# Softmax weights as exp(w - ln of the sum) on ScalarE, tap sums on TensorE in a reordered prologue, and a tiled linear rest, in a fused convolution and maxout kernel

## The chip, the cores and the metric

The kernel runs on one core of a Trainium2 chip. The metric is the device time of one execution in microseconds (us), given as a median over several executions. The core has five engines, each of which is given its instructions in program order: TensorE (PE in the profile, its weight loads PEld), VectorE (DVE), ScalarE (ACT), GpSimd (POOL) and SyncE (SP, which here only issues DMAs). Each execution is classed as fast or slow against the others of its kernel.

## The reference, cut to what matters

```python
w = np.exp(weight_gen - max)                      # (8, 4160, 8 heads, 7 taps)
w = w / (sum over taps + 1e-09)
out[b,s,h,:] = sum over k of w[b,s,h,k] * x_pad[b, s + k, h, :]     # 24 values per head
y  = out.reshape(33280, 192)
h1 = y @ w1                                       # 192 -> 1024
h2 = y @ w2
return np.maximum(h1, h2) @ w_out                 # 1024 -> 192
```

Both kernels use max(h1, h2) = h1 + relu(h2 - h1). They multiply y by wd = w2 - w1, take the relu, multiply by w_out, and add y times w10 = w1 @ w_out, which is a linear path of width 192. The inputs are small enough that neither subtracts the maximum.

## The kernel before

A sequence is laid out over 16 partitions, so that each of the 128 partitions holds 260 consecutive positions ("columns"). Work goes in chunks of 16 columns, and each chunk in two units of 8 for TensorE. Per chunk ScalarE does one exp. VectorE does the sums, the reciprocal, the weights written in pairs, the product with seven shifted copies of x, and three adds. A DMA transposes y. TensorE then runs, for a unit, four "slots", each with two of the eight slices of the hidden layer and two output columns of the unit before it.

```python
def exp(ci):
    ...
    nc.scalar.activation(out=e_t, in_=wg_ts.pop(ci), func=AF.Exp)

def conv(ci):
    ...
    nc.vector.reduce_sum(out=sum_t, in_=_sub(e_t, 0, [[K, TH], [1, K]]), axis=AX.X)
    nc.vector.reciprocal(out=rec_t, in_=sum_t)
    nc.vector.tensor_tensor(                                   # weights, each twice
        out=_sub(en_t, 0, [[2, TH], [2 * TH, K], [1, 2]]),
        in0=_sub(e_t, 0, [[K, TH], [1, K], [0, 2]]),
        in1=_sub(rec_t, 0, [[1, TH], [0, K], [0, 2]]), op=ALU.mult)
    nc.vector.tensor_tensor(out=m_t, in0=..., in1=..., op=ALU.mult)   # the product
    if ci + 2 < len(CHUNKS):
        load(ci + 2)
    ...                                                        # three adds, y_t
...
def out_first(u, i):                                           # the linear rest
    ...
    nc.tensor.matmul(op[:, 0:2 * D], lhsT=yt[:, (3*i + 1)*P:(3*i + 2)*P], rhs=w10R, ...)
...
for u in range(NU + 1):
    while queued < NCH and queued <= UNITS[min(u + 3, NU - 1)][0]:
        exp(queued)                                            # three units ahead
        conv(queued)
        queued += 1
    if u == 0:
        transpose(0)
    if u + 1 < NU:
        transpose(u + 1)
    for i in range(4):
        ...                                                    # one slot
```

The exp of a chunk is issued three units before TensorE needs it.

The softmax here doesn't subtract the row's maximum and nothing guards it: scores larger than these inputs give would overflow.

## Time and profile before

The time is 477.56 us (three runs, 477.13 to 477.79). The table gives, for the profiled execution, what the argument uses; the prediction shows the lines themselves and says how to read them.

| | busy us | share of the 476.3 us span |
|---|---|---|
| TensorE | 427.1 | 90% |
| VectorE | 418.6 | 88% |
| ScalarE | 336.5 | 71% |
| time of one chunk of 16 columns on VectorE | 25.61 | |
| time of one chunk on TensorE, when it doesn't wait | 25.25 | |

A share near 100% after the prologue on two engines at once means that neither can be helped alone: shortening one gains at most the difference to the other.

### The profile page before, as it was taken

To read this page: it belongs to the slowest core of one execution; us is meant where nothing else is said; L and a number is where in the kernel's file an instruction comes from. 1 tells how busy PE (TensorE), PEld (TensorE's weight loads), DVE (VectorE), ACT (ScalarE), POOL (GpSimd) and SP (SyncE) were. 2 spreads that over 40 slices of the span, in tenths; PEclk is the share of its full clock that TensorE was granted. 3 is DMA by queue.
4 is the path that set the end of the run, shared out by engine and by line. 5 is a ranking of instruction groups with operands and counts; after the bars stand their busy time and mean duration, and the time that the engine had idled before them with its cause. 6 is when DMAs were issued, how large, how long until landed. Compare 5 with 4: busy or idle time off the path is not lost.

```text
span 476.3 us, 8155 instructions
## 1 busy us (share of the span) xinstructions
PE 427.1 (90%) x3606; PEld 271.5 (57%) x3606; DVE 418.6 (88%) x136; ACT 336.5 (71%) x437; POOL 22.1 (5%) x46
## 2 busy tenths in 40 slices
PE   0087695599999999999999999989999999999997
PEld 0054353366666666666666666656666666666675
DVE  2949999999999999999999999999999999997000
ACT  1266374287877878787878787867878787777773
POOL 3000000000000000000000000000000000000000
PEclk9999698599999999999999999999999999999999
DMA  8945745546574737467585747384736537273212
GB/s 168 261 107 104 170 120 129 133 93 169 131 175 123 199 107 174 150 139 190 131 200 125 206 85 219 76 192 109 200 109 139 172 67 200 43 200 100 83 67 100
DMA packets 62131, 67.47 MB, mean 142 GB/s; under 512 B 52329, under 2 KB 53609, under 8 KB 60304
## 3 DMA queue, kind: packets, MB, share of 16 engines
q1 hardware_dynamic: 57792, 41.12, 31.1%
q0 software_dynamic: 4304, 25.84, 24.9%
q8 instruction: 28, 0.46, 0.4%
q14 instruction: 7, 0.06, 0.0%
HBM read 46.58 MB, written 25.56 MB: 151 GB/s over the span
## 4 chain that ended last, share of the span: by engine, by line
PE 81%; DVE 11%; DMA 5%; SPq 1%; ACT 1%; issue 0%; POOLq 0%
PE op_ps L292 34%; PE hdp L243 22%; PE hdp L258 13%; PE op_ps L279 7%; DVE m_t L138 5%; PE op_ps L287 4%; DMA wso<-in_moe_w_out_dram 3%; DVE m_t L149 2%; DMA yt<-y_t 2%; DVE m_t L151 1%; DVE en_t L130 1%; PE pw L211 1%; DVE y_t L154 1%; DMA wg_t<-in_weight_gen_dram 1%; DVE sum_t L125 1%; DVE rec_t L127 1%
## 5 line engine op out<-in xcount | busy, mean ns | idle before, releaser
L269 ACT ACTIVATE rd_t<-hdp 128x1024 bf16<-128x1024 f32 (+1 forms) x272 | 267.5, 986 | 112.0 <-PE hdp L258 77.2
L292 PE MATMUL op_ps<-wo,rd_t 128*128 128x192 bf16 x2080 | 216.6, 248 | 0.0
L292 PEld LDWEIGHTS <-rd_t 128*128 128x128 bf16 x2080 | 177.8, 99 | 23.7 <-issue 0.9
L138 DVE TENSOR_TENSOR m_t<-xb_t,en_t 128x21504 bf16<-128x21504 bf16 (+2 forms) x19 | 185.0, 9738 | 5.5 <-DMA xb_t<-zero_t 4.9
L243 PE MATMUL hdp<-yt,wdE 128*128 128x512 bf16 (+1 forms) x272 | 101.6, 374 | 20.8 <-DMA yt<-y_t 18.3
L243 PE MATMUL hdp<-yt,wdO 128*128 128x512 bf16 (+1 forms) x272 | 101.5, 373 | 0.0
L258 PE MATMUL hdp<-yt,wdR 64*128 64x512 bf16 (+1 forms) x544 | 81.6, 375 | 1.1 <-ACT rd_t L269 1.1
L149 DVE TENSOR_TENSOR m_t<-m_t 128x9216 bf16<-128x9216 bf16 (+2 forms) x19 | 81.0, 4263 | 0.7
L303 ACT COPY o_t<-op_ps 128x384 f32<-128x384 f32 x130 | 61.6, 474 | 2.5 <-PE op_ps L292 2.3
L151 DVE TENSOR_TENSOR m_t<-m_t 128x6144 bf16<-128x6144 bf16 (+2 forms) x19 | 55.0, 2894 | 0.7
L258 PEld LDWEIGHTS <-wdR 64*128 64x128 bf16 x544 | 16.2, 94 | 58.1 <-issue 57.5
L279 PE MATMUL op_ps<-w10R,yt 128*128 128x384 bf16 x130 | 44.0, 339 | 0.0
L279 PEld LDWEIGHTS <-yt 128*128 128x128 bf16 x130 | 12.4, 96 | 53.1 <-issue 52.8
L243 PEld LDWEIGHTS <-wdE 128*128 128x128 bf16 x272 | 26.8, 99 | 22.0 <-DMA yt<-y_t 19.6
L287 PEld LDWEIGHTS <-yt 128*128 128x128 bf16 x260 | 25.7, 99 | 14.8 <-issue 0.6
L130 DVE TENSOR_TENSOR en_t<-e_t,rec_t 128x1792 bf16<-128x1792 bf16 (+2 forms) x19 | 33.4, 1755 | 0.7
L287 PE MATMUL op_ps<-w10E,yt 128*128 128x192 bf16 x130 | 32.2, 248 | 0.0
L287 PE MATMUL op_ps<-w10O,yt 128*128 128x192 bf16 x130 | 32.2, 248 | 0.0
L154 DVE TENSOR_TENSOR y_t<-m_t 128x3072 bf16<-128x3072 bf16 (+2 forms) x19 | 29.0, 1527 | 0.7
L243 PEld LDWEIGHTS <-wdO 128*128 128x128 bf16 x272 | 26.8, 99 | 3.6 <-issue 3.4
L125 DVE TENSOR_REDUCE sum_t<-e_t 128x128 f32<-128x896 bf16 (+2 forms) x19 | 17.9, 944 | 9.9 <-ACT e_t L115 9.9
L105 POOL DMA_DIRECT2D xb_t<-in_x_dram x18 | 9.5, 529 | 333.4 <-DVE m_t L138 333.4
(29 smaller groups left out, 69.0 us busy)
## 6 DMA issues: line engine op xcount, KB each, us to landing
out_dram<-o_t SPq DMA_DIRECT2D x31, 768.0 KB, 3.9
xb_t<-in_x_dram POOLq DMA_DIRECT2D x14, 1056.0 KB, 7.8
wg_t<-in_weight_gen_dram POOLq DMA_DIRECT2D x14, 448.0 KB, 6.1
xb_t<-in_x_dram POOLq DMA_DIRECT2D x3, 672.0 KB, 7.9
wg_t<-in_weight_gen_dram POOLq DMA_DIRECT2D x4, 224.0 KB, 5.5
wso<-in_moe_w_out_dram SPq DMA_DIRECT2D x1, 768.0 KB, 13.5
out_dram<-o_t SPq DMA_DIRECT2D x2, 384.0 KB, 3.6
yt<-y_t SPq DMA_TRANSPOSE x34, 3.8
```

Of the source, the lines that this page charges most:

```text
L130: nc.vector.tensor_tensor(out=_sub(en_t, 0, [[2, TH], [2 * TH, K], [1, 2]]), in0=_sub(e_t, 0, [[K, TH], [1, K], [0, 2]]), in1=_sub(rec_t, ...
L138: nc.vector.tensor_tensor(out=m_t, in0=_sub(xb_t, 0, [[D, K], [1, n]]), in1=_sub(en_t, 0, [[2 * TH, K], [2, TH], [0, D // H // 2], [1, 2]] ...
L149: nc.vector.tensor_tensor(out=m_t[:, 0:3 * n], in0=m_t[:, 0:3 * n], in1=m_t[:, 3 * n:6 * n], op=ALU.add)
L151: nc.vector.tensor_tensor(out=rows(m_t, 2, 2, 0), in0=rows(m_t, 2, 2, 0), in1=rows(m_t, 5, 2, 1), op=ALU.add)
L154: nc.vector.tensor_tensor(out=y_t, in0=m_t[:, 0:n], in1=m_t[:, 2 * n:3 * n], op=ALU.add)
L243: nc.tensor.matmul(hd_ts[u, f][:, j * 512:j * 512 + N], lhsT=wd[kind][:, f * P:(f + 1) * P], rhs=_sub(yt_ts[u], 2 * j * P, [[3 * P, n // 2 ...
L258: nc.tensor.matmul(hd_ts[u, f][:, j * 512:j * 512 + N], lhsT=wd["R"][r, f * P:(f + 1) * P], rhs=_sub(yt_ts[u][r, :], P, [[3 * P, n // 2], ...
L269: nc.scalar.activation(out=_sub(rd_ts[u], f * 1024, [[512, 2], [1, N]]), in_=_sub(hd_ts.pop((u, f)), 0, [[512, 2], [1, N]]), func=AF.Relu,)
L279: nc.tensor.matmul(op[:, 0:2 * D], lhsT=yt[:, (3 * i + 1) * P:(3 * i + 2) * P], rhs=w10R, start=True, stop=False, skip_group_check=True,)
L287: nc.tensor.matmul(op[:, sl], lhsT=yt[:, (3 * i + 2 * j) * P:(3 * i + 2 * j + 1) * P], rhs=(w10E, w10O)[j], start=False, stop=False, skip_ ...
L292: nc.tensor.matmul(op[:, sl], lhsT=rd[:, f, j * 512 + i * P:j * 512 + (i + 1) * P], rhs=wo[:, f * D:(f + 1) * D], start=False, stop=(f == ...
L303: nc.scalar.copy(out=o_ts[u][:, 2 * i * D:2 * (i + 1) * D], in_=op_ts.pop((u, i))[:, 0:2 * D])
```

## The change

Its intent is to take work off both full engines and to start TensorE sooner. VectorE loses the reciprocal and the paired product: ScalarE takes ln of the sums, VectorE subtracts it from the logits, and ScalarE writes exp of the result, reading each value twice. TensorE's linear rest, one matmul with a half-zero weight of 384 columns, becomes two 64-row matmuls side by side. In the prologue the taps of the first 16 columns are summed by matmuls with the identity, which leave y already transposed. "Batch" below is a chunk of 16 columns, counted from 0. From batch 1 on, y goes by DMA transpose, one for each unit; batch 2 is the first whose product is done in one instruction.

```diff
-        nc.vector.reciprocal(out=rec_t, in_=sum_t)
-        nc.vector.tensor_tensor(out=_sub(en_t, ...), in0=_sub(e_t, ...), in1=_sub(rec_t, ...), op=ALU.mult)
+    def ln(b):
+        nc.scalar.activation(out=s_ts[b], in_=s_ts[b], func=AF.Ln)
+    def shift(b):                       # fp32, 896 elements
+        nc.vector.tensor_tensor(out=wg, in0=wg, in1=s_ts.pop(b), op=ALU.subtract)
+    def weights(b, part=None):          # part 0: taps 0 to 3, part 1: taps 4 to 6
+        nc.scalar.activation(out=..., in_=_sub(wg_ts[b], ..., [[1, k1 - k0], [K, N], [0, 2]]), func=AF.Exp)
 ...
+    def sum_transpose(u):               # prologue only
+        for k in range(nb):
+            for t in range(K):
+                nc.tensor.matmul(ps[:, k * P:(k + 1) * P], lhsT=m_ts[b][...], rhs=ident, ...)
 ...
-            op[:, 0:2 * D], lhsT=yt[:, (3 * i + 1) * P:(3 * i + 2) * P], rhs=w10R,
+        for j in range(2):
+            r = slice(64 * j, 64 * j + 64)
+                lhsT=yt_ts[u][r, (3 * i + 1) * P:(3 * i + 2) * P], rhs=w10[r, 2 * D:3 * D],
 ...
+    extras = {
+        (1, 0): lambda: (weights(1), start_mul_1(), load_x(2, 0, 16), load_wg(4, nc.gpsimd)),
+        ...
+        (2, 0): lambda: exp_sum(3),
+        (2, 1): rest_1,
+        (2, 3): lambda: transpose(4),
+        ...
+    }
+    def extra(u, i):                    # after slot i of unit u
+        ...
+        if i == 0 and second and b + 1 < NB:
+            c, w = b + 1, BATCHES[b + 1][1]
+            mul(c, 0)                   # then shift(c + 1), red(c + 2), the adds, the loads
+            ...
+        if i == 1 and u + 1 < NU:
+            transpose(u + 1)
+        if second and b + 2 < NB:       # second: the second unit of batch b
+            if i == 1:
+                weights(b + 2, 0)
+            if i == 3:
+                weights(b + 2, 1)
+        if second and i == 3 and b + 3 < NB:
+            ln(b + 3)
```

The evictions of the output are also grouped (four of 768 elements per batch in place of eight of 384).

## The prediction

> **What bounds the kernel now.** I read the busy shares first, then the busy time in slices and by stage, then the groups of instructions kept apart by shape, then the timeline around one wait. Busy shares and slices (tenths of each fortieth of the span):
>
> ```profile
> PE 427.1 (90%) x3606; PEld 271.5 (57%) x3606; DVE 418.6 (88%) x136; ACT 336.5 (71%) x437; POOL 22.1 (5%) x46
> ...
> PE   0087695599999999999999999989999999999997
> ...
> DVE  2949999999999999999999999999999999997000
> ...
> PEclk9999698599999999999999999999999999999999
> ```
>
> TensorE and VectorE are both full from about 90 us on, so the slices cannot say which of them sets the pace. The groups give the work of one chunk of 16 columns on VectorE (line, shapes, count, busy us, mean ns):
>
> ```profile
> L138 DVE TENSOR_TENSOR m_t<-xb_t,en_t 128x21504 bf16<-128x21504 bf16 x14 | 159.0, 11359 | 0.5
> ...
> L149 DVE TENSOR_TENSOR m_t<-m_t 128x9216 bf16<-128x9216 bf16 x14 | 69.4, 4958 | 0.5
> ...
> L151 DVE TENSOR_TENSOR m_t<-m_t 128x6144 bf16<-128x6144 bf16 x14 | 47.0, 3357 | 0.5
> ...
> L154 DVE TENSOR_TENSOR y_t<-m_t 128x3072 bf16<-128x3072 bf16 x14 | 24.6, 1758 | 0.5
> ...
> L130 DVE TENSOR_TENSOR en_t<-e_t,rec_t 128x1792 bf16<-128x1792 bf16 x14 | 28.4, 2025 | 0.5
> ...
> L125 DVE TENSOR_REDUCE sum_t<-e_t 128x128 f32<-128x896 bf16 x14 | 15.1, 1078 | 0.0
> ...
> L127 DVE RECIPROCAL rec_t<-sum_t 128x128 f32<-128x128 f32 x14 | 13.3, 953 | 0.5
> ```
>
> They sum to 25.49 us. In the timeline of VectorE the product L138 starts at 267.89, 293.51 and 319.12, so a chunk takes 25.61, with no waits. For TensorE I take its repeating slot (a unit of 8 columns has four, a chunk eight). The timeline of TensorE around the one late wait:
>
> ```profile
> 313.22 0.34 PE L279 MATMUL op_ps<-w10R,yt 128*128 128x384 bf16 x1
> ...
> 316.38 0.34 PE L279 MATMUL op_ps<-w10R,yt 128*128 128x384 bf16 x1
> ...
> 317.80 0.82 PE L292 MATMUL op_ps<-wo,rd_t 128*128 128x192 bf16 x8
> 320.38 0.39 PE L243 MATMUL hdp<-yt,wdE 128*128 128x512 bf16 x1 [1.76 <-DMA yt<-y_t]
> ```
>
> A slot is 316.38 - 313.22 = 3.16 us, a chunk 25.25. TensorE is 0.36 faster per chunk than what feeds it, so from its cold start at 88.41 (0.61 us matmuls in place of 0.38, some 3 us lost) it catches up until it waits at 320. **VectorE sets the pace**, by a hair, and the start costs about 50 us: at 88.41 only 24 of 260 columns are through, which at 12.6 us per 8 columns is 38 us of work. From y_t ready (315.04) to the first matmul on it (320.38) is 5.3 us; at 84.5 to 88.41 it is 3.9.
>
> **What the Trainium skill says.** "VectorE: DVE Perf Modes", section "The perf-mode tier table", gives bf16 tensor_tensor two elements per cycle, fp32 tensor_tensor and any reduce one. The trace agrees: at that page's 0.96 GHz, 21504 / 2 is 11.2 us (11.36 seen), and the reduce of 896 is 0.93 (1.08 seen). "ScalarE: Activation LUTs", section "What ACT_TABLE_LOAD costs", gives an ACTIVATE with immediates 186 ns + 0.833 ns per element, with 93 ns overlap between neighbours: 0.93 us for 896 (0.942 seen). Its section "Table sets: the hidden batching unit" puts exp and ln in one set, so Ln should add no reload; before has one load, no run yet shows two functions. "TensorE: Matmul & The Clock Gate", Part 1, has the clock fall to half after an idle window of 3.4 us. The trace agrees in kind: idle for 6.18 and 10.34 us was followed by about 6 us of 0.6 us matmuls, idle for 1.76 was not.
>
> **The change, per 16 columns.** VectorE loses the reciprocal (0.95) and the pairing product (2.03). It gains an fp32 subtract of 896 elements, one per cycle, estimated 1.08 like the reduce of the same size. Product and adds keep their element counts. So 25.61 - 2.98 + 1.08 = 23.7 us.
>
> TensorE: the 384-column linear matmul (about 0.165 us) becomes two 64-row matmuls of 192 columns side by side (about 0.082, the step of the 192-column ones). The mode switches stay (about 0.1 us each, two in a slot: L243 to L258 steps 0.31 in place of 0.21). Slot 3.16 - 0.08 = 3.08; eight are 24.6.
>
> ScalarE: 16 relus of 1.02, exp 0.94 and eight evictions of 0.474 were 21.1. Evictions become four of 768 elements, estimated 0.79 each; new are ln (128 elements, 0.29) and the paired exp in two parts (1024 and 768 elements: 1.04 and 0.83). Sum 22.7 us, below TensorE. But each extra stands just before a slot with an eviction, in order: relu, extra, relu, eviction, relu is 0.35 us late for its two buffers by my count, of which about 0.2 reaches TensorE. Two such inside a batch: 25.0 us.
>
> If that were all, TensorE would set 25.0 against 25.6: 0.6 x 14 = 8 us won.
>
> **The wait that I expect to take its place.** Before, the exp that starts VectorE's work for a chunk is issued three units ahead. In the change the weights of batch b+2 come from ScalarE after the last relu of batch b, and ScalarE runs in program order. Call F(b) the time when TensorE starts batch b, G(b) when it has issued it (F + 25.0). The last relu starts about 0.55 before G, the next activation 0.93 later, part two takes 0.83: weights ready at G(b) + 1.25. Then VectorE does 23.7 (product, the next batch's subtract, a reduce, adds over all 16 columns, so y comes out at the end). Then the transpose: 3.9. So F(b+2) = F(b) + 25.0 + 1.25 + 23.7 + 3.9 = F(b) + 53.85: **26.9 us per batch**, above TensorE (25.0) and VectorE (23.7). The loop does not depend on how the kernel starts. Every two batches TensorE waits 3.85 us and VectorE about 6.4. Fourteen batches cost 14 x (26.9 - 25.6) = 18 us more.
>
> **The prologue**, estimated from the durations of before. Loading 16 columns of weight_gen first gives exp at about 5.5, reduce, ln, subtract to 9.1, paired exp to 9.75, product of 4 columns (2.96) to 12.7. The seven taps then sum on TensorE (42 matmuls, 4 to 5 us cold) to 17.5. The matrices start at 7.7, not 6.9, but without the loads beside them, and land by 17 (21 before). VectorE subtracts to 18.5, the shifted copies via TensorE and ScalarE take to 21, one cast and one exp to 23. The hidden layer of unit 0 runs 23 to 28 (1.28 per two f, as unit 0 before; it was 31.4), then tap sums (3.4), transposes (3.5), copy (1.9), w1 w_out (2.0 and 0.65) to 39. Slot 0 of unit 1 ends with the paired exp: first half ready at about 42.7. From there VectorE has an unbroken 49 us: 5.8 + 5.1, reduce 1.1, 5.8, 1.1, 1.1, 5.1, then 11.4 + 2.2 + 10.2. It is free for batch 3 at 91.7, and batch 2 starts at about 90.5. Column 32 starts at about 88.4 + 12.6 + 3 = 104 before. So the prologue wins some 13.5 us.
>
> **Sum.** F(3) = 91.7 + 23.7 + 3.9 = 119.3. F(15) = 119.3 + 6 x 53.85 = 442.4. G(15) = 467.4. The last 4 columns: four slots of 0.86 + 1.56 = 9.7, the last output 3.2, eviction and store 3.4 as now: 483.7, and 1.2 for the time above the span: 484.9. Roughly, -13.5 from the start, +18 from the loop, +3 as the tail no longer runs on a lead of three units.
>
> **Rivals.** (1) TensorE stays full at 25.0, because the weights come early enough or I misread which batch they serve. For it: a scheduler who saw the waits would have removed them, and one wait hides in slack easily. Against it: exp in the trace of before starts at 255.69, 280.93 and 306.22, in program order at the unit where it is issued. This gives 484.9 - 27 = 458. (2) The waits of 3.85 us exceed the 3.4 us idle window often enough to halve the clock: up to 3 us more for each of six, 490 to 500. The 1.76 us wait that did no harm says little here. (3) ScalarE becomes the bound, through reads of 0-stride pairs slower than one per cycle: double the 1.9 us and relu falls behind, 495. The VectorE pairing product, with such reads, kept 1792 / 0.96 = 1.87 (2.03 seen), which speaks against. (4) The loads of the prologue land late: each us there moves the end by one.
>
> **Range and chances.** The loop gives 485, give or take 5 for the prologue and 6 for six loops (1 us each: transpose 3.0 to 5.3, slot 3.05 to 3.15). I weigh it 4 to 1 against rival 1, so I set 482 and a range of 462 to 496. Faster than 468: almost only rival 1, 0.22. Slower than 487.1: 0.32. Between: 0.46.
>
> **What would show it.** Right: TensorE waiting on the transposed y about 3.9 us before every second batch, VectorE idle before its product with ScalarE's weights named as the cause, product starts 53.9 apart over two, no wait of the product in before. Also: VectorE 23.7 per batch, slot 3.08, batch 2 at 90. Wrong: TensorE full from 90 us on (rival 1), clock below 1 after 100 us (rival 2), the paired exp over 1.04 us (rival 3), TensorE's first hidden matmul after 26 us (rival 4).

## The result, and the profile after

The changed kernel took 500.76 us (four runs, 498.27 to 502.37) against 477.68 for the kernel before in the same rounds. The ratio is 1.048, with a 95% interval of 1.043 to 1.053: it is slower. Ratios here are the mean time of one kernel's fast runs over that of the other's in the same rounds, so they are not quite the ratio of the medians quoted. The results of both kernels are correct, and so are those of all experiments.

The page of the changed kernel, busy shares and slices (tenths of each fortieth of the 496.5 us span):

```profile
PE 444.1 (89%) x3942; PEld 289.4 (58%) x3942; DVE 374.5 (75%) x115; ACT 362.6 (73%) x428; POOL 32.4 (7%) x63
...
PE   0789858997999979997999979997999979998996
...
DVE  4737989598977989498968989398959989497000
...
PEclk9989989999899989999999979999899989999999
```

VectorE's work fell from 418.6 to 374.5 us, as intended. What is new is the pattern: TensorE and VectorE, which were solid 9s, both dip to 7 or less at a steady distance, and the clock dips with some of them. Neither engine is full, so a loop of waits sets the pace.

The groups by shape, for what the softmax became (count, busy us, mean ns, then idle before it and who ended it):

```profile
L145 DVE TENSOR_TENSOR m_t<-xb_t,en_t 128x21504 bf16<-128x21504 bf16 x14 | 159.0, 11358 | 59.2 <-ACT en_t L134 59.2
...
L121 DVE TENSOR_TENSOR wg_t<-wg_t,sum_t 128x896 f32<-128x896 f32 x16 | 17.3, 1084 | 0.4 <-ACT sum_t L117 0.4
...
L134 ACT ACTIVATE en_t<-wg_t 128x1024 bf16<-128x1024 f32 x14 | 15.9, 1136 | 0.0
...
L134 ACT ACTIVATE en_t<-wg_t 128x768 bf16<-128x768 f32 x14 | 12.4, 883 | 0.0
```

The product is as long as before (11358 ns), but it now stands idle for 59.2 us in all, always for the paired weights that ScalarE writes in L134. Before, that idle time was 0.5. The table of waits gives the two ends of the loop (us in total, times, longest):

```profile
DVE m_t L145 <- ACT en_t L134: 73.2, 17, 11.2
...
PE hdp L203 <- DMA yt<-y_t: 26.4, 8, 5.4
```

VectorE waits for ScalarE, and TensorE waits for the transposed y. ScalarE's weights stand in its program order behind relus that wait for TensorE, which closes the loop. The chain that ended last passes through all of it between 120 and 152 us, with TensorE's batch in the place of the dots (start, duration; "issue" is time in which nothing that the profile shows was waited for):

```profile
120.60 3.69 DMA yt<-y_t
...
150.34 1.02 ACT rd_t L229
151.37 0.79 ACT en_t L134
152.16 0.02 issue
152.18 0.04 DVE m_t L145
```

VectorE's timeline shows two batches of it (start, duration, and in brackets the idle time before):

```profile
97.13 11.36 DVE L145 TENSOR_TENSOR m_t<-xb_t,en_t 128x21504 bf16<-128x21504 bf16 x1 [5.72 <-ACT en_t L134]
...
118.78 1.76 DVE L164 TENSOR_TENSOR y_t<-m_t 128x3072 bf16<-128x3072 bf16 x1
122.32 11.36 DVE L145 TENSOR_TENSOR m_t<-xb_t,en_t 128x21504 bf16<-128x21504 bf16 x1 [1.78 <-ACT en_t L134]
...
152.18 11.36 DVE L145 TENSOR_TENSOR m_t<-xb_t,en_t 128x21504 bf16<-128x21504 bf16 x1 [6.46 <-ACT en_t L134]
```

From 97.13 to 152.18 is 55.05 us for two batches, where VectorE works 23.4 us in each. Before, two chunks took 51.2. TensorE's timeline at the start of four of its batches that follow a wait:

```profile
124.34 0.39 PE L203 MATMUL hdp<-yt,wdE 128*128 128x512 bf16 x1 [3.15 <-DMA yt<-y_t]
...
179.37 0.61 PE L203 MATMUL hdp<-yt,wdE 128*128 128x512 bf16 x1 [3.14 <-DMA yt<-y_t]
...
234.39 0.61 PE L203 MATMUL hdp<-yt,wdE 128*128 128x512 bf16 x1 [3.12 <-DMA yt<-y_t]
...
454.16 0.39 PE L203 MATMUL hdp<-yt,wdE 128*128 128x512 bf16 x1 [2.10 <-DMA yt<-y_t]
```

A wait of some 3.1 us stands before every second batch, and batches that wait start 55.0 us apart. The 0.61 us matmuls are at half clock. Where the first one is still 0.39 (124.34), the clock falls just after. The stretches of 2 us show this (bounds, length, busy us of PE, PEld, DVE, ACT and POOL with counts, then granted clock, DMA share, GB/s):

```profile
122.00:124.00 2.00, 0.00 (x0) 0.00 (x0) 1.68 (x1) 0.48 (x2) 0.54 (x1) 1.00 1.34 207
124.00:126.00 2.00, 1.66 (x8) 0.40 (x8) 2.00 (x1) 0.38 (x1) 0.00 (x0) 0.69 0.62 201
126.00:128.00 2.00, 2.00 (x13) 1.57 (x12) 2.00 (x1) 1.33 (x2) 0.00 (x0) 0.50 0.00 0
```

After the idle stretch, TensorE is busy again, but at a clock of 0.50 until about 128. At all six waits of 3.11 to 3.20 us (before batches 3 to 13, every second one) the clock fell to half, between 0.64 us before the wait's end and 1.05 us after it; at the one of 2.10 before 454.16 it did not.

Last, the prologue. The chain that ended last passes through the first DMA transpose (start, duration):

```profile
58.31 12.31 DMA yt<-y_t
```

The timeline of all engines there:

```profile
58.30 0.53 POOL L97 DMA_DIRECT2D xb_t<-in_x_dram  x1 [27.44 <-DVE m_t L145]
...
70.66 0.61 PE L203 MATMUL hdp<-yt,wdE 128*128 128x512 bf16 x1 [5.45 <-DMA yt<-y_t]
```

Its source had been written at 51.3, but it was issued at 58.31, in the same instant as a load of x, and took 12.31 us. TensorE waited 5.45 us for it, and the loop carries that on: VectorE was free at 91.42, but waited 5.72 us, until 97.13, for the weights that stand behind batch 1.

Adding up the profiled execution against the prediction's own sum: batch 3 started at 124.34 and not at 119.3 (+5.0), the six loops to batch 15 took 454.16 - 124.34 = 329.8 and not 323.1 (+6.7), and the tail 42.3 and not 41.3 (+1.0). Together they are the 12.8 us by which the span (496.5) exceeds the predicted 483.7. (The median of 500.76 lies 2.5 us above this execution, whose granted clock was the highest of the four, 0.966.)

### The profile page after: what moved, and what is told of

The parts are those of the page before. It is cut to its first block, busy times and chain, and to the rows that moved or that the text cites. A ratio compares the mean times of both kernels' runs of the same rounds, so it can differ in the third digit from the quotient of the medians.

```text
span 496.5 us, 8822 instructions
## 1 busy us (share of the span) xinstructions
PE 444.1 (89%) x3942; PEld 289.4 (58%) x3942; DVE 374.5 (75%) x115; ACT 362.6 (73%) x428; POOL 32.4 (7%) x63
## 4 chain that ended last, share of the span: by engine, by line
PE 48%; DVE 15%; issue 14%; ACT 12%; DMA 9%; POOL 0%; SPq 0%; ACTq 0%; POOLq 0%
PE op_ps L256 18%; PE hdp L203 13%; PE hdp L218 8%; DMA yt<-y_t 8%; ACT rd_t L229 7%; DVE m_t L162 6%; DVE m_t L163 4%; PE op_ps L251 4%; ACT en_t L134 2%; PE yps L184 2%; DVE y_t L164 2%; ACT o_t L268 2%; PE op_ps L242 1%; DVE wg_t L121 1%; DVE sum_t L114 1%
## 5 line engine op out<-in xcount | busy, mean ns | idle before, releaser
L218 PE MATMUL hdp<-yt,wdR 64*128 64x512 bf16 (+1 forms) x560 | 89.2, 378 | 3.5 <-ACT rd_t L229 1.9
L251 PE MATMUL op_ps<-w,yt 128*128 128x192 bf16 x260 | 66.2, 255 | 0.0
L218 PEld LDWEIGHTS <-wdR 64*128 64x128 bf16 x560 | 21.3, 94 | 70.1 <-issue 69.5
L251 PEld LDWEIGHTS <-yt 128*128 128x128 bf16 x260 | 25.4, 98 | 52.7 <-issue 38.8
L268 ACT COPY o_t<-op_ps 128x768 f32<-128x768 f32 x65 | 51.8, 797 | 3.0 <-PE op_ps L256 2.8
L134 ACT ACTIVATE en_t<-wg_t 128x1024 bf16<-128x1024 f32 (+5 forms) x36 | 33.1, 930 | 1.2 <-DVE wg_t L121 1.2
L242 PE MATMUL op_ps<-w,yt 64*128 64x192 bf16 x260 | 33.3, 248 | 0.2 <-ACT w L394 0.2
L184 PE MATMUL yps<-ident,m_t 128*128 128x128 bf16 x168 | 12.0, 241 | 11.4 <-POOL gate L322 11.4
L114 DVE TENSOR_REDUCE sum_t<-e_t 128x128 f32<-128x896 f32 (+1 forms) x17 | 17.6, 1037 | 3.1 <-ACT e_t L109 3.1
L242 PEld LDWEIGHTS <-yt 64*128 64x128 bf16 x260 | 13.4, 96 | 10.2 <-issue 2.3
```

The costliest lines, as they stand in the source:

```text
L134: nc.scalar.activation(out=_sub(en_ts[b, o], k0 * N * 2, [[2 * N, k1 - k0], [2, N], [1, 2]]), in_=_sub(wg_ts[b], o * WGC + k0, [[1, k1 - k ...
L218: nc.tensor.matmul(hd_ts[u, f][:, j * 512:j * 512 + N], lhsT=wd["R"][r, f * P:(f + 1) * P], rhs=_sub(yt_ts[u][r, :], P, [[3 * P, n // 2], ...
L242: nc.tensor.matmul(op_ts[u, i // 2][:, at:at + D], lhsT=yt_ts[u][r, (3 * i + 1) * P:(3 * i + 2) * P], rhs=w10[r, 2 * D:3 * D], start=(i % ...
L251: nc.tensor.matmul(op[:, at:at + D], lhsT=yt[:, (3 * i + 2 * j) * P:(3 * i + 2 * j + 1) * P], rhs=w10[:, j * D:(j + 1) * D], start=False, ...
L268: nc.scalar.copy(out=_sub(o_ts[u], 4 * g * D, [[2 * D, 2], [D, 2], [1, D]]), in_=_sub(op_ts.pop((u, g)), 0, [[D, 2], [512, 2], [1, D]]))
```

## The experiments

The theory after the result: the pace is set by the loop "weights on ScalarE, 23.4 us of VectorE, transpose, TensorE's batch, weights", which spans two batches because the weights' second half is issued in the last slot of a batch. Rivals: the half clock is the main loss and the loop only shows it; the prologue's late transpose is the main loss; or the new work is in truth no cheaper than the old. The first four runs shared a chip and its runs of the kernel before (477.93), the next four another set (477.92), the last four a third (477.23).

**1. The second half of the weights one slot earlier** (slot 2 in place of 3).

```diff
             if i == 1:
                 weights(b + 2, 0)
-            if i == 3:
+            if i == 2:
                 weights(b + 2, 1)
```

> Only the second half of the paired exp moves, from slot 3 to slot 2 of a batch's second unit (3.07 us earlier). Theory (a two-batch loop: weights, 23.4 us of VectorE, 3.8 us of transpose, 25.2 us of TensorE): each loop shortens by 3.07, from 55.0 to about 52, the waits of 3.15 us before every second batch shrink to about 0.1 to 0.3, and the half clock behind them (1.4 us each) goes too: seven times 4.4, so 500.8 - 31 = 470, give or take 4. Rival (the engines are simply full, or ScalarE's extra work delays the relus): nothing is removed, 499 to 502. If the clock is not a result of the wait, only 22 us go: 479.

Measured: 474.00 us (473.40 to 474.59), ratio 0.992 (0.990 to 0.994), at the upper end of what I expected. Moving one instruction of 0.88 us by one slot is worth 26.8 us. The waits before every second batch shrank to 2.12 us or less (not to 0.3), as TensorE's timeline at the same place shows:

```profile
124.15 0.39 PE L203 MATMUL hdp<-yt,wdE 128*128 128x512 bf16 x1 [2.12 <-DMA yt<-y_t]
```

The granted clock stayed at 1.00 in every stretch looked at from 120 to 132 and from 170 to 300 us. So the idle time of 2.12 us did not cost the clock here, and those of 3.1 us did before. The length alone does not decide it, as the last section shows.

**2. The same half one slot later** (the first slot of the next batch).

```diff
+        if o == 0 and i == 0 and 3 <= b + 1 < NB:
+            weights(b + 1, 1)
         if second and b + 2 < NB:
             if i == 1:
                 weights(b + 2, 0)
-            if i == 3:
-                weights(b + 2, 1)
```

> The second half of the paired exp moves one slot later, behind slot 0 of the next batch's first unit. Theory: it then waits for TensorE's start of that batch, so the loop spans one batch in place of two: F(b+1) + 4.4 to 5.6 + 23.4 + 3.8 = 31.6 to 32.8 us per batch in place of 27.5, fourteen times: 500.8 + 58 to 75 = 559 to 576, with a TensorE wait of some 6 us in every batch. Rival (full engines): a move of 0.8 us of ScalarE work by one slot changes nothing, 499 to 503; a plain delay of 3 us per two batches would give 520.

Measured: 575.18 us (574.79 and 575.57), ratio 1.204, slower. TensorE now waits 5.1 to 6.7 us before every batch from 3 on, not every second one, and each time starts at half clock:

```profile
163.23 0.61 PE L203 MATMUL hdp<-yt,wdE 128*128 128x512 bf16 x1 [5.83 <-DMA yt<-y_t]
```

Products start 33.0 to 33.6 us apart (136.06, 169.66, 202.69). The loop closes within one batch now, since the weights of the next batch wait for the first slot of this one. With experiment 1 this settles that the time follows the place of this one instruction.

**3. TensorE kept busy in the waits**: 12 matmuls of 512 columns, with results that are overwritten, before batches 3, 5 and so on. The loop stays; the idle time goes.

```diff
+                if i == 0 and UNITS[u][1] == 0 and UNITS[u][0] % 2 == 1 and UNITS[u][0] > 2:
+                    hd_ts[u, 0] = pps_h.tile([P, 1024], FP32, name="hdp", tag="hd")
+                    for _ in range(12):
+                        nc.tensor.matmul(hd_ts[u, 0][:, 0:512], lhsT=wd["E"][:, 0:P], rhs=wd["O"][:, 0:512], start=True, stop=True, ...)
                 hid_main(u, 2 * i)
```

> Twelve matmuls of 512 columns without use (2.6 us) are put in front of batches 3, 5, ... 15, where TensorE waits for 3.15 us; their results are overwritten. Theory that the wait halves the clock: the starts of these batches stay where they are relative to the loop, the mean clock rises from 0.96 to 0.98 or more, 1.4 us are won in each of six to seven: 490 to 492, and the spread of the runs (498 to 502) shrinks. Rival (the clock falls for another reason, or not at a cost): 500 as before; and if the waits were not idle at all, 12 x 0.213 = 2.6 us are added seven times: 518.

Measured: 488.03 us (five runs, 486.88 to 491.04), ratio 1.020 (1.018 to 1.023), which is unclear against the 2% bound. The clock was 1.00 in all stretches from 100 to 400 us, and two batches took 53.4 to 53.6 us, against 55.0. So the half clock costs about 1.5 us per loop, 9 us over six loops, and work that does nothing recovers it. The medians differ by 12.7, more than expected (490 to 492). The mean granted clocks place the rest: the changed kernel's other executions ran at 0.954 to 0.961, lower than its profiled one (0.966), and those of this kernel at 0.986 to 0.989, above its profiled one (0.979, the slowest of the five). Span times mean clock is 477.5 to 480.3 us over the four executions of the changed kernel and 479.0 to 481.9 over the five of this one, so by this estimate the lost clock is all that separates the two. What is left, 53.5 us over two batches, is the loop at full clock, and it is still slower than the 51.2 of before.

**4. Both halves early** (slots 0 and 1).

```diff
-            if i == 1:
+            if i == 0:
                 weights(b + 2, 0)
-            if i == 3:
+            if i == 1:
                 weights(b + 2, 1)
```

> Both halves of the paired exp move by two slots and more (slots 0 and 1 of the second unit, from 1 and 3); nothing else changes. Theory: the loop has about 3 us to spare, TensorE runs without waits from batch 1 on at 25.2 us per batch: batch 16 starts at 95.84 + 14 x 25.2 = 448.6 in place of 478.8, so the time is 500.8 - 30 = 470, the same as with the half in slot 2 or 1 to 2 us less, VectorE busy 23.4 of 25.2. Rival (full engines): 499 to 502. Against before (477.7) 1 to 2 per cent faster at best: what the softmax change is worth once its wait is gone.

Measured: 463.52 us (three fast runs, 461.36 to 464.79; a fourth, of 469.15, was slow), ratio 0.969 (0.966 to 0.973): faster than before, and some 6 us below what I expected. TensorE does not wait from 100 us on, and VectorE's timeline shows a loop of one batch:

```profile
144.27 11.36 DVE L145 TENSOR_TENSOR m_t<-xb_t,en_t 128x21504 bf16<-128x21504 bf16 x1 [1.30 <-ACT en_t L134]
...
168.98 11.36 DVE L145 TENSOR_TENSOR m_t<-xb_t,en_t 128x21504 bf16<-128x21504 bf16 x1 [1.31 <-ACT en_t L134]
```

A batch takes 24.71 us, now TensorE's own pace. That is less than the 25.2 that the same batch takes in the changed kernel when it isn't cold. I put the difference down to the first half no longer standing just before an eviction on ScalarE, but did not isolate it.

**5. The first DMA transpose issued earlier** (after slot 0 of the second unit, not after slot 3).

```diff
-        (2, 0): lambda: exp_sum(3),
+        (2, 0): lambda: (transpose(4), exp_sum(3)),
         (2, 1): rest_1,
-        (2, 3): lambda: transpose(4),
```

> Only the first DMA transpose (unit 4, batch 1) moves: it is issued in slot 0 of unit 2 in place of slot 3, so no longer behind a store that waits for unit 1 and no longer beside the loads of batch 3 that start at 58.3. y is ready at 51.3. Theory: it lands by 57, not 70.66 (12.3 us from issue); batch 1 starts when TensorE is ready at 65.3, with no half clock: batch 2 starts 6.5 to 7 us earlier (about 89), the product of batch 3 at 91 to 92 in place of 97.1, and all that follows moves by 5.5 to 6: about 495. Rival (the loop absorbs it, or another wait comes in its place): 499 to 502.

Measured: 495.77 us (495.44 to 496.10), ratio 1.037 (1.035 to 1.040). It is slower than before still. Batch 3 started at 119.69 in place of 124.34, and the median fell by 5.0 us (the profiled execution by 2.8: in it the clock fell to half after a wait of 2.22 us before batch 15). The loop is unchanged, with 55 us for two batches. So the late transpose was worth some 5 us, all of it in the prologue, and it cannot be the main loss.

**6. Both mends, 4 and 5.**

> Early halves (as in the fourth kernel) and the early first transpose together. Theory: the two gains are on the same chain and add: 470 - 6.5 = 463 to 464, TensorE without a wait of over 0.5 us from 40 us on but for VectorE at batch 2 or 3 (its products are free for batch 3 at 91.3, so batch 3 can't start before 118.5; TensorE would want it at 115: up to 3.5 us lost there, 466). Rival: one of them hides the other, 470.

Measured: 462.83 us (462.23 to 463.54), ratio 0.969 (0.966 to 0.971), faster. The gains don't add: it is 0.7 us under the fast runs of experiment 4, whose range contains it. With TensorE through batch 2 sooner, VectorE is still in batch 3, and TensorE waits there instead (2.80 us at 119.89, again with half clock after it). Shorter waits cost the clock in other runs (1.95 us in experiment 7), and longer ones did not (3.49 us in experiment 9).

**7. Other slots for ScalarE's additional work.** The transpose of experiment 5; the weights, exp and ln moved to slots 0 and 2, so that none stands before an eviction; and VectorE's block issued a unit earlier in the program.

```diff
-        if (o, i) == (0, 1) and b + 4 < NB:
-            exp_sum(b + 4)
-        if i == 0 and second and b + 1 < NB:
+        if i == 0 and b + 1 < NB and (second if b == 1 else o == 0):
 ...
+        if (i == 2 and o == 0 and 2 <= b < NB - 2) or (i == 0 and second and b == 1):
+            weights(b + 2, 0)
+        if second and i == (2 if b == 1 else 0) and b + 2 < NB:
+            weights(b + 2, 1)
+        if second and i == 2:           # exp_sum(b + 4) and ln(b + 3)
```

> As the sixth, and each extra of ScalarE now stands in a slot that an eviction does not follow (0 or 2, in place of 1 or 3); to that end VectorE's work for a batch is issued one unit earlier. Theory that an extra in front of an eviction makes the relu late and TensorE lose 0.3 us two times per batch: a batch takes 8 x 3.07 = 24.6 in place of 25.2, 0.6 x 14 = 8 us: 456 to 458. Rival (ScalarE has slack, 73 per cent busy): 464, as the sixth.

Measured: 469.08 us (468.02 to 470.78), ratio 0.982 (0.979 to 0.985), classed as unclear. It missed what I expected by some 12 us. The timelines of SyncE, GpSimd and TensorE show why (the bracket of the GpSimd line says that the load waited for the product):

```profile
326.08 2.48 SPq L171 DMA_TRANSPOSE yt<-y_t  x1
...
326.73 0.54 POOL L97 DMA_DIRECT2D xb_t<-in_x_dram  x1 [10.86 <-DVE m_t L145]
...
336.53 0.39 PE L203 MATMUL hdp<-yt,wdE 128*128 128x512 bf16 x1 [1.17 <-DMA yt<-y_t]
```

The transpose is in SyncE's order behind a store of the output, so it was issued 12.2 us after its y was ready (313.88 in VectorE's timeline). By then the next product had ended and let the load of x go, 0.65 us later. The transpose took 10.40 us beside it, and TensorE waited 1.17 us. It is the same collision as in the prologue of the changed kernel, now in nearly every batch: between 100 and 400 us the median transpose took 8.3 us, against 4.3 in the changed kernel. The chain that ended last holds six of them with 9.65 to 10.40 us, each issued 0.6 to 0.9 us before the load of x.

**8. The kernel before with the tiled linear rest alone** (and the output columns moved in PSUM as it needs).

```diff
-        nc.tensor.matmul(op[:, 0:2 * D], lhsT=yt[:, (3*i + 1)*P:(3*i + 2)*P], rhs=w10R, ...)
+        for j in range(2):
+            r = slice(64 * j, 64 * j + 64)
+            nc.tensor.matmul(op[:, j*512:j*512 + D], lhsT=yt[r, (3*i + 1)*P:(3*i + 2)*P], rhs=w10R[r, :], ...)
```

> The kernel before with one part of the change alone: the 384-column linear matmul becomes two 64-row ones of 192 columns. Theory (VectorE sets the pace of before, 25.61 per chunk against TensorE's 25.25): TensorE's slot falls from 3.16 to 3.07 us, and the time by 0 to 3 us only (a little at the start and in the tail of 36 us that TensorE runs after VectorE has ended): 475 to 478. Rival (TensorE sets the pace): 0.085 x 4 x 30 = 10 us less, 467.

Measured: 475.74 us (473.86 to 476.70), ratio 0.995 (0.991 to 1.000). VectorE keeps its pace, and TensorE's gain turns into a wait, in the timeline of all engines:

```profile
240.01 0.39 PE L242 MATMUL hdp<-yt,wdE 128*128 128x512 bf16 x1 [0.78 <-DMA yt<-y_t]
...
240.80 11.36 DVE L138 TENSOR_TENSOR m_t<-xb_t,en_t 128x21504 bf16<-128x21504 bf16 x1
```

The product before this one started at 215.18, so a chunk still takes 25.6 us. This confirms the first step of the prediction: VectorE set the pace of the kernel before, and a faster TensorE alone gains next to nothing.

**9. Experiment 7 with each transpose issued two slots earlier**, ahead of the store.

```diff
-        if i == 1 and u + 1 < NU:
+        if (u, i) in ((4, 1), (5, 1)):
             transpose(u + 1)
+        if i == 3 and 5 <= u < NU - 2:
+            transpose(u + 2)
```

> As the seventh, but each DMA transpose is issued two slots earlier, before the store and the loads of its batch. In the seventh the transpose stood behind a store in the queue although its input had been ready for 12 us, was issued at 326.08 just as the loads of x began at 326.73, and took 10.4 us. Theory (a transpose beside the loads takes 10 us in place of 4): the waits of about 1 us before each batch go (9.1 us in all), a batch takes 24.6: 466.1 - 8 = 458 span, 459 to 461 time. Rival (the seventh is slow because ScalarE's extras hurt more in slots 0 and 2): stays at 468.

Measured: 460.23 us (459.20 to 461.16), ratio 0.964 (0.961 to 0.966). This is the fastest version, 3.6% under the kernel before. After the start of batch 3 TensorE doesn't wait for y. Two lines of VectorE's timeline give the period:

```profile
236.05 11.36 DVE L145 TENSOR_TENSOR m_t<-xb_t,en_t 128x21504 bf16<-128x21504 bf16 x1 [1.20 <-ACT en_t L134]
260.65 11.36 DVE L145 TENSOR_TENSOR m_t<-xb_t,en_t 128x21504 bf16<-128x21504 bf16 x1 [1.20 <-ACT en_t L134]
```

That is 24.60 us per batch, the eight slots of 3.08 that the prediction worked out. It also confirms the cause found in 7: the arithmetic is the same, and only the transposes moved.

**10. Experiment 6 with the old softmax** (reciprocal and paired product on VectorE) from batch 4 on, its exp issued early.

```diff
+            if c >= 4:
+                old_softmax(c)      # reduce, reciprocal, paired product on VectorE
             mul(c, 0)
 ...
```

> As the sixth (early halves, early first transpose), but from batch 4 on the weights are made as before the change: exp once on ScalarE, then sum, reciprocal and pair product on VectorE, with the exp issued early. VectorE then does 25.6 us per batch against TensorE's 24.7. Theory: VectorE sets the pace again, 12 batches x 0.9 = 11 us: 474, give or take 2, TensorE waiting some 0.9 us for y in each batch, VectorE without waits. That is what moving the softmax to ScalarE is worth. Rival (moving it is worth nothing, only the order counts): 463.

Measured: 470.15 us (468.63 to 472.28), ratio 0.985 (0.982 to 0.988). Products start at 219.29, 244.91 and 270.52, a period of 25.6 us as before, and TensorE waits up to 1.8 us for a batch. With the loop out of the way, the softmax on ScalarE is worth 7.3 us against experiment 6, less than the 11 expected. The two ran on different chips, whose medians of the kernel before differ by 0.7 us.

**11. Experiment 6 with the linear rest untiled** (two 128-row matmuls with zero-padded weights).

```diff
-                lhsT=yt_ts[u][r, (3 * i + 1) * P:(3 * i + 2) * P], rhs=w10[r, 2 * D:3 * D],
+                lhsT=yt_ts[u][:, (3 * i + 1) * P:(3 * i + 2) * P], rhs=w10z[:, j * D:(j + 1) * D],
 ...
```

> As the sixth, with the linear rest not tiled: two 128-row matmuls of 192 columns with zero-padded weights, 0.165 us of TensorE in place of 0.085. Theory: TensorE sets the pace of the sixth, so all of it shows: 0.085 x 130 pairs = 10 to 11 us: 473. In the kernel before, the same part alone gave 2.2. Rival (worth little here too): 465.

Measured: 469.78 us (469.12 to 470.52), ratio 0.984 (0.982 to 0.986). A batch takes 25.26 us (218.26, 243.52, 268.78), and the tiling is worth 7.0 us here (10 to 11 were expected; the chips differ as in experiment 10), where it was worth 2 in the kernel before. The same part has a different worth in another balance.

**12. Experiment 9 with the adds of batch 3 in two halves**, so that the first half of y is ready sooner.

```diff
-            step = 8 if c == 2 else w
+            step = 8 if c in (2, 3) else w
```

> As the ninth, and the adds of batch 3 are done in two halves of 8 columns, so that its first y is ready 5 us earlier. Theory: the one wait left after the start (1.7 us before batch 3 in the seventh, plus up to 1.4 of half clock) goes: 1 to 3 us below the ninth, 457 to 459. Rival: it only moves to batch 4, the same as the ninth.

Measured: 460.33 us (459.57 to 461.57), ratio 0.964 (0.962 to 0.967), the same as 9. The wait at batch 3 went, the one of 3.49 us inside batch 2 shrank to 1.77, one of 1.95 us appeared before batch 2, and the spans are 457.8 and 458.4. It is not shown to gain anything.

## Why the prediction was right or wrong

I predicted 482 us with a range to 496, and gave "within 2%" the largest chance, 0.46. It came out at 500.76, slower by 4.8% and outside the range.

**What bounds the kernel before: right.** Experiment 8 shows it, since TensorE got faster and the time stayed.

**The cost of the parts: right to a few tenths.** VectorE per batch was estimated at 23.7 and measured at 23.41 (97.13 to 120.54). The fp32 subtract was put at 1.08 and is 1.084. A slot was put at 3.08 and is 3.07 (137.30 to 140.37 in the chain). The paired reads were put at 1.04 and 0.83 and are 1.136 and 0.883. That is above rival 3's sign of 1.04, but only by 0.05 to 0.1 us and not double; whether the pairs cost it, or the stride of seven at which the values lie, no run separates. Ln caused no reload, as expected: the trace has one table load, of 1.28 us.

**The loop: right in kind, too small in size.** The prediction named the wait, its cause, the weights after the last relu, and its period of two batches. Experiments 1, 2 and 4 show it by moving only the instructions that write the weights: 575, 501, 474 and 464 us as they go earlier. The step that failed is the term F(b+2) = F(b) + 53.85. It measured 55.0. Of its parts, VectorE's 23.4 and the way from y to the matmul of 3.80 were slightly under the estimate (23.7, 3.9). The part from TensorE's start to VectorE's product was over it: 25.0 + 1.25 = 26.25 was predicted, and from 124.34 to 152.18 it was 27.84. After a batch start without a long wait it was 26.48 (95.84 to 122.32). The difference of 1.4 us is the half clock. I had it as rival 2, and left it out of the sum, although my own loop put the wait at 3.85 us, above the 3.4 us window that I quoted: by its own premise the prediction should have charged it. The waits came out shorter, at 3.1 us, below that window, and cost the clock all the same, which is rival 2's sign (clock below 1 after 100 us). Experiment 3 takes the half clock away and leaves the loop at 53.5, close to the term as predicted.

**The prologue: right in kind, too optimistic.** It was to win 13.5 us and won about 8. TensorE began earlier than predicted (18.6, not 23), so rival 4 in its form of late matrices did not happen, and the first product of batch 1 started at 40.2, not 42.7. But the step "transposes take 3.9" failed for the first of them, which took 12.31 beside the load of x. Batch 2 started at 95.84 in place of 90.5 and batch 3 at 124.34 in place of 119.3. Experiment 5 gives back 5.0 us.

**The blend: wrong.** The sum was 484.9. I pulled it to 482 with one part in five for rival 1, that a scheduler would have hidden the wait (a mean of 484.9 and 458 with these weights would be 479.5), and set the top of the range at 496, although rival 2 alone reached 500. Nothing in the diff spoke for rival 1: the issue order is plain in it. The top should have held the sum and rival 2 together.

**Where the gain went.** VectorE did get faster by 2.2 us per batch, and TensorE's eight slots by some 0.65, which shows in full only in experiment 9. The kernel before paid for throughput, and the changed one pays for latency: 27.5 us per batch on a loop in which no engine is full. With the weights earlier, the same parts give 3.6% (experiment 9), and the softmax and the tiling are worth about 7 us each when one is taken out (experiments 10 and 11, against 6).

**What stays open.** The 0.5 us per batch between 25.2 and 24.71 in experiment 4, for which the cause is only argued; and how little TensorE must have worked for the clock to fall, which the runs give only roughly (last section).

## What to carry to other kernels

When work moves from a full engine to one with spare time, look at where it stands in that engine's program order: if it is behind something that waits for the end of the pipeline, the move makes a loop, and the period of the loop, not the sum of the work, sets the pace. Write the loop out with every term, and add to each wait what follows it, such as a slower clock. Issue small work that starts a long chain first, and issue a transpose as soon as its source is ready, ahead of stores in its queue and before the next large load starts.

## What the Trainium skill lacked or had wrong

- "TensorE: Matmul & The Clock Gate", Part 1, gives the fall to half clock after at least one idle window of about 3.4 us. Here TensorE's records show idle times of 3.11 to 3.20 us, shorter than that, and at six of six the clock fell. But no length of one wait decides it: waits of 1.77 (experiment 12), 1.95 (7), 2.22 (5) and 2.80 us (6) cost the clock, and waits of 2.10 (changed kernel), 2.12 (1), 2.67 (11) and 3.49 us (9) did not. In the clock records of the changed kernel the half clock begins at 124.78, 179.39 and 234.01, which is 16 steps of 3.41 us apart each time, and lasts one step, or two. What tells the cases apart after the first 60 us is how long TensorE was busy in the step of 3.41 us before: after 0.44 us (changed kernel, 121.37 to 124.78), 1.20 (5), 1.26 (6), 1.46 (7) and 1.65 (12) the clock fell, and after 1.47 (9), 1.60 (11), 1.71 (changed kernel) and 2.17 (1) it did not. (Within the first 60 us it fell after up to 2.70 us too, in experiment 4, so busy time is not the whole measure.) So the step need not be idle, and a wait split between two steps can be harmless: whether a wait of 2 or 3 us costs the clock depends on where it falls. In the loop here one cost some 1.4 us.
- "DMA: Bandwidth & Descriptors", section "Issuing engines are not separate DMA queues", says that DMAs from all engines share the same 16 DMA engines and interleave. The trace agrees, in that a transpose issued by SyncE is slow beside a load issued by GpSimd, but the page gives no size for it. After the first, the transposes on the chain of the changed kernel, with no load of x beside them, took 3.65 to 3.89 us; where a load of x was issued within a microsecond, a transpose took 12.31 (changed kernel) and 8.56 to 10.40 (experiment 7). The load of x need not be alone in this: the changed kernel's second transpose, at 66.88, took 12.79 beside two loads of weight_gen, a store and only the end of a load of x.
- "ScalarE: Activation LUTs", section "What ACT_TABLE_LOAD costs", has a formula for the time of an ACTIVATE, but no term for an input of which each value is read twice through a zero stride, the values lying seven apart. Such reads took 1136 ns for 1024 elements and 883 ns for 768, where the formula gave the prediction 1040 and 830.
